# One DMA pipe in a list-scheduled transformer kernel's plan, tile rates by pairs of half entries, and layer 2 biases in one operation

## The chip, the cores and the metric

The kernel runs on one core of a Trainium2 chip. The metric is the device time of one launch in microseconds, smaller is better. All times are of that core. TensorE multiplies matrices into PSUM, VectorE (DVE), ScalarE (ACT) and GpSimd (POOL) work elementwise, and SyncE (SP) issues DMA transfers only.

## The reference

Two layers with the same weights are applied to 2048 tokens of width 448 in bf16. A layer is an attention block with 16 heads of 28 columns, and then a block of a token mixer and an MLP of width 1792; both add to their input:

```python
x = x + _A_ref(_layernorm(x), A_wqkv, A_wo)
x = x + _B_ref(_layernorm(x), B_w1, B_w2, B_w3, B_w4)
# twice
_A_ref: q, k, v = heads of x @ wqkv;  p = softmax(q k^T * 28**-0.5);  (p v) @ wo
_B_ref: h = gelu(layernorm(x) @ w1), its four column quarters moved by
        +1, -1, +2, -2 tokens;  x1 = x + h @ w2
        x1 + gelu(layernorm(x1) @ w3) @ w4
```

## The kernel before, in words

**A program from a planner.** The kernel is written as some hundred Python generators (their names begin with `t_`). Each yields operations with an engine, an estimated duration, and what they read and write, or waits for and gives signals. While the kernel is built, the class `Sched` (from line 185) simulates the engines with these estimates and picks one operation after the other (`run`, line 385); the class `Plan` (line 43) turns what each reads and writes into semaphore waits. What reaches the chip is one fixed list of instructions for each engine, which works through it in order. An estimate never runs on the chip, it only decides the order; any change of an estimate or of a priority can move operations anywhere in the program. For a DMA the planner knows the issuing engine's issue time (`iss`) and the time until the data are there (`t`); line 505 handles both.

**Attention.** Two layers are cut into 68 segments: the lists in `ORDER` have 8 entries for layer 1 and 9 for layer 2, each a stretch of queries (512 or 256 of them) against a stretch of key tiles, and each is done for four groups `g` of four heads. Two neighbouring segments, `si // 2`, make half an entry; there are 34 such pairs. The scores of one 128-key tile, one head and 512 columns fill one PSUM bank; there are 2048 such tiles. `t_scores` (line 1474) gives them to TensorE (matmul at line 1353) in units of three and two tiles alternately: banks 0 to 2, then banks 3 and 4. `t_exp` (line 1576) lets ScalarE take the exponential of a unit in one instruction (line 1591) out of PSUM into the ring `PT`. A unit may be scored when the exponential two units before it is through. `t_pv` (line 1603) multiplies the result with the values (matmuls recorded at line 802). The wider projections and the output matrices go through a helper that records them at line 811.

**Tiles for VectorE.** Some tiles are not given to ScalarE. VectorE takes their exponential by a polynomial in five operations: the first reads PSUM (`d_first`, line 1435), four more make up `d_chain` (lines 1462, 1464, 1466 and 1469). Such a tile comes in two kinds. A *ring* tile stands in bank 2, in the place of the third tile of a unit of three, so that ScalarE's exponential of this unit has two tiles; the unit that uses bank 2 next waits until VectorE has read it (`dx`). Any other VectorE tile is scored into one of the two banks kept for miscellaneous work (6 and 7), beside a full unit. How many there are is set by `R_RATE` (ring) and `D_RATE`, which have one rate per layer and query chunk. A rate is asked for at lines 1476 to 1508: a tile some 5 to 8 key blocks ahead is taken while the segment's count is below rate x blocks x 4, VectorE's planned load is low and buffers are free.

**Softmax bias.** The exponent's shift comes from the keys' largest norm so far. `t_bias` (line 1288) computes it for one layer, one stretch of keys and one head group, in four small VectorE operations of 128x1 (one at line 1300); when an entry begins with later keys, `t_fct` (line 1311) and `t_db` (line 1321) compute the difference of two such biases and a factor for what was summed before, and `t_qp` (line 1370) adds the difference to the queries.

**Loads and transposes.** `t_load` (line 824) issues the inputs; on the POOL queue (records at lines 848 to 858) it loads `wo`, `w1` and `w2` when segment `LSEG[1]` starts and `w3`, `w4` when `LSEG[2]` starts. `t_setup2` (line 981) zeroes `wo_pad` on POOL when segment `LSEG[0]` starts. `load_xT` (line 1120) waits for four normalized token tiles in DRAM (`xnd`) and loads them transposed by one DMA on SP's queue (line 1123); `tr_dma` (line 1013, DMA at line 1015) does the same for one tile from SBUF. The transposed tokens `xT` feed the projections of queries, keys and values.

**Mixer and MLP.** `t_mixA` (line 1787) and `t_mixB` (line 1927) follow the output projection. ScalarE's gelu needs another table than its exponential, so a gelu among exponentials costs two table loads: it runs over seven blocks of 512 columns at once (line 2019, `vaug` 128x3584). `tanh_gelu` (line 1833) is the other way: GpSimd and VectorE form the argument, ScalarE takes a tanh from the exponential's table (line 1839), VectorE finishes it. `TANHW` says by layer and first tile of the chunk which of the two a chunk's MLP uses, 0 for gelu.

**Fillers.** `keep_pe_busy` (line 324) puts matmuls on constants into TensorE's list (line 2065) where the plan leaves the engine idle.

The program's last part is what depends on the last segments: output projection, mixer and MLP of the last tokens, and the stores (`t_final`, line 2059). `RANK` and `Q_LEAD` are the priorities of the projections, norms, mixers and MLPs, and the lead that a chunk's query projection gets over its first use.

## Time and profile before

| what | value |
| --- | --- |
| median of three runs (lowest, highest) | 1064.53 us (1062.19, 1065.12) |
| the profiled execution's own time | 1063.28 us |
| its span, first to last instruction | 1061.5 us |
| mean granted TensorE clock | 0.992 |
| busy: PE, DVE, ACT, POOL | 990.9, 680.6, 1007.3, 306.0 us |
| largest group on ACT (line 1591) | 802 instructions, 910.4 us |
| filler matmuls (line 2065) | 3212 |

The span is the time from the first to the last instruction of the profiled execution; its own time is 1.8 us longer. An engine's busy time is the sum of the stretches in which it ran anything. A group is written as line, engine, operation, output and input, with the number of instructions, their busy time, the mean duration of one in ns, and then the idle time ahead of them with what ended most of it. Such durations can overlap their neighbours on the same engine, so that count times mean may exceed the busy time. A row of the timeline has start, length, engine, and in brackets the wait that ended there. Where several places are compared, a table by stretches of the span gives each engine's busy time in them. SPq and POOLq are the queues in which these two engines issue DMAs.

### The profile page before, as it was taken

The page shows a single profiled execution, that of the slowest core. Times are in us where ns is not written, and L with a number is a line of the kernel's source. Part 1 is how long each engine was busy: PE and PEld are TensorE (multiplying, and loading weights), DVE is VectorE, ACT ScalarE, POOL GpSimd, SP SyncE. Part 2 cuts the span into 40 slices and gives each one's busy share as a digit, 9 for nine tenths or more (in the row PEclk, how much of TensorE's full clock was granted, in tenths as well). Part 3 has the DMA queues.
Part 4 walks back from the last instruction along what each step waited for, and adds up shares of the span by engine and source line. Part 5 has one row for each costly group of instructions (what it writes and reads, how often), then busy time and mean ns, then how long its engine had stood idle before and what let it go on. Part 6 is the DMA issues. An engine that isn't in the chain of part 4 may idle for free.

```text
span 1061.5 us, 35381 instructions
## 1 busy us (share of the span) xinstructions
PE 990.9 (93%) x15980; PEld 410.0 (39%) x15983; DVE 680.6 (64%) x1365; ACT 1007.3 (95%) x913; POOL 306.0 (29%) x507
## 2 busy tenths in 40 slices
PE   8898998999999999999999989998989999899998
PEld 4332342333424334434432333343333343444465
DVE  7674797788568757776457445747778536565442
ACT  7998999999999999999999999999999999999952
POOL 2342112434232304453234111103554300432111
PEclk9999999999999999999999999999999999999999
DMA  4547232402121103231132114334412110121000
GB/s 117 130 117 202 76 72 68 62 22 37 21 75 41 33 12 86 63 52 23 33 78 74 44 52 129 104 76 116 74 23 32 32 39 25 34 66 25 12 21 24
DMA packets 96443, 64.22 MB, mean 61 GB/s; under 512 B 68580, under 2 KB 85172, under 8 KB 96292
## 3 DMA queue, kind: packets, MB, share of 16 engines
q1 hardware_dynamic: 92916, 53.88, 21.1%
q0 software_dynamic: 3376, 8.09, 2.8%
q8 instruction: 125, 2.05, 0.8%
q14 instruction: 26, 0.21, 0.1%
HBM read 28.03 MB, written 16.76 MB: 42 GB/s over the span
## 4 chain that ended last, share of the span: by engine, by line
ACT 72%; PE 20%; DMA 3%; DVE 3%; issue 1%; SPq 1%; POOL 0%; DVEq 0%
ACT PT L1591 66%; PE ps L811 11%; PE ps L1353 4%; PE ps L802 3%; ACT h2T L2019 2%; DMA xT<-xnd 2%; ACT fb L1839 1%; PE ps L2065 1%; ACT L2019 1%; DMA xT<-xn 1%; ACT L1591 1%; DVE fb L1462 0%; DMA rT<-ub 0%; DMA PT<-in_A_wqkv_dram 0%; SPq L1015 0%
## 5 line engine op out<-in xcount | busy, mean ns | idle before, releaser
L1591 ACT ACTIVATE PT<-ps 128x1024 bf16<-128x1024 f32 (+1 forms) x802 | 910.4, 1340 | 15.5 <-PE ps L1353 14.8
L1353 PE MATMUL ps<-qT,kT 32*128 32x512 bf16 (+1 forms) x2560 | 315.2, 341 | 36.8 <-ACT PT L1591 28.4
L802 PE MATMUL ps<-PT,vaug 128*32 128x512 bf16 (+1 forms) x2491 | 250.9, 342 | 0.8 <-ACT PT L1591 0.5
L1353 PEld LDWEIGHTS ps<-qT,kT 32*128 32x128 bf16 x2560 | 80.6, 91 | 317.6 <-ACT PT L1591 285.1
L811 PE MATMUL ps<-xT,w 128*32 128x512 bf16 (+4 forms) x2368 | 160.9, 345 | 5.8 <-DMA xT<-xn 4.0
L2065 PE MATMUL ps<-ident 128*32 128x256 bf16 x3212 | 145.9, 279 | 4.2 <-DVE hT L1820 2.4
L802 PEld LDWEIGHTS ps<-PT,vaug 128*32 128x32 bf16 x2491 | 74.2, 95 | 93.4 <-issue 76.8
L2065 PEld LDWEIGHTS ps<-ident 128*32 128x32 bf16 x3212 | 90.8, 98 | 31.9 <-issue 13.1
L811 PE MATMUL ps<-w,h2T 128*32 128x448 bf16 x1288 | 90.5, 358 | 5.7 <-ACT h2T L2019 5.7
L1696 POOL TENSOR_TENSOR otn<-ub,fb 128x512 bf16<-128x512 f32 (+1 forms) x35 | 39.9, 1139 | 187.7 <-DMA fb<-rscr 187.7
L1998 DVE CAST h2T<-ps 128x384 bf16<-128x384 f32 (+1 forms) x84 | 52.2, 622 | 50.8 <-PE ps L811 50.0
L811 PEld LDWEIGHTS ps<-xT,w 128*32 128x32 bf16 (+1 forms) x2368 | 64.6, 96 | 50.1 <-issue 27.2
L1138 POOL TENSOR_TENSOR sq<-kT 128x512 bf16<-128x512 bf16 (+2 forms) x32 | 31.2, 981 | 94.7 <-DVE kT L1152 80.4
L1837 POOL TENSOR_TENSOR fb<-hT 112x512 f32<-112x512 bf16 (+1 forms) x36 | 37.8, 1054 | 61.7 <-DVE hT L1820 53.7
L811 PEld LDWEIGHTS ps<-w,h2T 128*32 128x32 bf16 x1288 | 36.0, 97 | 34.9 <-issue 15.2
L811 PE MATMUL ps<-xT,wk_pad 128*32 128x512 bf16 (+2 forms) x576 | 44.6, 366 | 3.1 <-DMA xT<-xnd 3.0
L1923 POOL TENSOR_TENSOR x_res<-x_res,x1b 128x448 f32<-128x448 f32 x32 | 38.2, 1199 | 32.1 <-DVE xn L1010 32.1
L1435 DVE TENSOR_SCALAR yd<-ps 128x512 int32<-128x512 f32 x43 | 29.5, 687 | 25.6 <-PE ps L1353 25.2
L1138 POOL TENSOR_TENSOR sq<-qT 128x512 bf16<-128x512 bf16 x28 | 30.6, 1100 | 43.2 <-DVE qT L1187 36.2
L811 PE MATMUL ps<-wo_pad,otn 128*32 128x448 bf16 x512 | 39.5, 356 | 2.9 <-DVE x_res L1750 1.6
L811 PE MATMUL ps<-w,hT 112*32 112x448 bf16 x512 | 41.2, 355 | 0.5 <-DVE x1b L1908 0.5
L811 PE MATMUL ps<-xT,wq_pad 128*32 128x512 bf16 x448 | 39.3, 388 | 1.4 <-DMA xT<-xnd 0.9
(183 smaller groups left out, 1190.3 us busy)
## 6 DMA issues: line engine op xcount, KB each, us to landing
uscr<-ub SPq DMA_DIRECT2D x28, 256.0 KB, 2.0
ub<-uscr SPq DMA_DIRECT2D x28, 256.0 KB, 4.0
fb<-rscr SPq DMA_DIRECT2D x24, 256.0 KB
xnd<-xn SPq DMA_DIRECT2D x28, 128.0 KB, 2.1
x_res<-in_A_x_dram POOLq DMA_DIRECT2D x16, 224.0 KB, 2.7
xd<-x_res SPq DMA_DIRECT2D x16, 224.0 KB, 2.9
x_res<-xd SPq DMA_DIRECT2D x16, 224.0 KB, 3.6
out_dram<-obf SPq DMA_DIRECT2D x16, 112.0 KB, 1.7
```

What stands on the lines that cost most here:

```text
L802: return lambda e: e.matmul(out=out, lhsT=lhsT, rhs=rhs, start=start, stop=stop, **kw)
L811: r.append(e.matmul(out=out[c:c + w, :], lhsT=lhsT[:, c:c + w], rhs=rhs, start=start, stop=stop, tile_position=(0, c)))
L1138: return both("sq", 0.15 + NW * 0.0018, 0.07 + NW * 0.00104, lambda e: e.tensor_tensor(out=sq[:, si, 0:NW], in0=src, in1=src, op=ALU.mult) ...
L1353: yield op("pe", (0.005 + NW * 0.00042) / nc_, lambda e, i=i, kc=kc, j=j, g=g, a=a, NW=NW, bank=bank: e.matmul(out=ps[:, bank, i * NW:(i + ...
L1435: yield op("dve", c_ps(512), lambda e: e.tensor_scalar(out=y, in0=ps[:, bi(bank), :], scalar1=SCALE * L2E * FS, scalar2=-126.0 * FS, op0=A ...
L1591: yield op("act", 0.06 + n * w * 0.000833, lambda e, bk=bk, s0=s0, n=n, w=w: e.activation(out=PT[:, s0:s0 + n, 0:w], in_=ps[:, bk[0]:bk[0] ...
L1696: yield both("otn", 0.2 + NW * 0.0021, 0.07 + NW * 0.00104, lambda e: e.tensor_tensor(out=otn[:, g, 0:NW], in0=u, in1=rb[:, 0:NW], op=ALU. ...
L1837: yield both("z2", 0.2 + NW * 0.00165, 0.07 + NW * 0.00104, lambda e: e.tensor_tensor(out=f, in0=z, in1=z, op=ALU.mult), hk, [fk])
L1923: yield both("xx", 1.2, 0.54, lambda e: e.tensor_tensor(out=X, in0=X, in1=X1, op=ALU.add), [xk, ("x1b", s)], [xk], deps=[nop_])
L1998: ev = op("dve", c_ps(m * NW), lambda e, hr=hr, pv=pv: e.tensor_copy(out=hr, in_=pv), reads=[("ps", bi(b))], writes=hk, touch=[b])
L2019: yield op("act", c_act(len(fr_) * NW), lambda e, v=v: e.activation(out=v, in_=v, func=ACT.Gelu_apprx_tanh), reads=allk, writes=allk, tab= ...
L2065: return [e.matmul(out=ps[32 * c:32 * c + 32, bi(b), 0:256].rearrange("p (a n) -> p a n", n=128), lhsT=ident[:, 32 * c:32 * c + 32], rhs=i ...
```

## The change

Four things are changed, and a number of settings with them.

- The planner gets one DMA pipe (`self.pipe`). A DMA with a service time `svc` occupies it for so long, one after the other, and its data arrive at the pipe's end or later; with `hold` (the transposing loads) the issuing queue is held until the pipe is free. Most DMAs get such a time, issue times are 0.4 instead of 0.35 (1.25 instead of 1.2 for `tr_dma`), and the weight loads' estimates fall from 8, 16 and 18 us to 5. The same `svc` argument is added to the stores of `xn`, `x` and `u`, to their loads and to the load of `rscr`, which are left out below.
- `R_RATE` and `D_RATE` are keyed by the pair of segments, `si // 2`, with new values; `DRATE`, which nothing calls, goes. `RPRIO`, the planner's priority for reading a ring tile, goes from 0.5 to 1, and the farthest key block ahead from 7 to 8 (`DHI`, exclusive, 8 to 9).
- In layer 2 the biases of all four head groups are computed together (`t_bias4`), and so are the differences in `t_fct`; in layer 1 `t_bias` of every head group 1 to 3 keeps its priority, and that of group 0 gets the highest for all stretches of keys.
- The weight loads of `t_load` wait for the signal that `wo_pad` has been zeroed (`woz`), and `LSEG` goes from (4, 7, 9) to (5, 5, 7).

`TANHW` gets one entry set, and all of `RANK` and most of `Q_LEAD` have new values.

```diff
@@ -502,8 +503,14 @@
             if kw.get("port"):
                 self.port[eng] = (start, t_end)
             if dma:
-                self.cur[eng] = start + kw.get("iss", 0.35)
+                svc = kw.get("svc", 0.0)
+                self.cur[eng] = start + kw.get("iss", 0.4)
                 t_end = start + kw.get("dma_time", 3.0)
+                if svc:
+                    if kw.get("hold"):
+                        self.cur[eng] = max(self.cur[eng], self.pipe)
+                    self.pipe = max(self.pipe, start + 1.2) + svc
+                    t_end = max(t_end, self.pipe + 1.2)
             else:
                 self.cur[eng] = t_end
...
@@ -535,21 +542,21 @@
...
-R_RATE = {(0, 0): 0, (0, 1): 0.03, (0, 2): 0.01, (0, 3): 0.02, (0, 4): 0, (1, 0): 0, (1, 1): 0, (1, 2): 0, (1, 3): 0.01, (1, 4): 0}
+R_RATE = {(0,): 0, (1,): 0.03, (2,): 0.06, (3,): 0.01, (4,): 0, (5,): 0, (6,): 0, (7,): 0, (8,): 0.05, (9,): 0.05, (10,): 0.04, (11,): 0.04, (12,): 0.02, (13,): 0.03, (14,): 0, (15,): 0, (16,): 0.04, (17,): 0.04, (18,): 0, (19,): 0, (20,): 0.02, (21,): 0.08, (22,): 0, (23,): 0, (24,): 0.04, (25,): 0.04, (26,): 0, (27,): 0, (28,): 0.01, (29,): 0.01, (30,): 0, (31,): 0, (32,): 0.03, (33,): 0.03}
 RLO = 5
 RHI = 7
-RPRIO = 0.5
+RPRIO = 1
...
-DHI = 8
+DHI = 9
...
-Q_LEAD = {(0, 1): 10, (0, 2): 5, (0, 3): 6, (1, 0): 4, (1, 1): 8, (1, 2): 5, (1, 3): 9}
-D_RATE = {(0, 0): 0.11, (0, 1): 0.1, (0, 2): 0.07, (0, 3): 0, (0, 4): 0, (1, 0): 0.005, (1, 1): 0.105, (1, 2): 0.03, (1, 3): 0.02, (1, 4): 0}
...
+Q_LEAD = {(0, 1): 12, (0, 2): 6, (0, 3): 6, (1, 0): 12, (1, 1): 18, (1, 2): 6, (1, 3): 8}
+D_RATE = {(0,): 0.14, (1,): 0.135, (2,): 0.14, (3,): 0.145, (4,): 0.14, (5,): 0.185, (6,): 0.14, (7,): 0.135, (8,): 0.12, (9,): 0.155, (10,): 0.08, (11,): 0.05, (12,): 0.015, (13,): 0, (14,): 0.005, (15,): 0, (16,): 0.025, (17,): 0, (18,): 0.07, (19,): 0.12, (20,): 0.025, (21,): 0.04, (22,): 0.125, (23,): 0.105, (24,): 0.025, (25,): 0.04, (26,): 0.07, (27,): 0.105, (28,): 0.03, (29,): 0.03, (30,): 0.065, (31,): 0.05, (32,): 0.065, (33,): 0.095}
...
-TANHW = {(0, 0): 0, (0, 3): 0, (0, 7): 0, (0, 11): 0, (0, 13): 0, (1, 0): 0, (1, 3): 0, (1, 7): 0, (1, 11): 0}
+TANHW = {(0, 0): 0, (0, 3): 0, (0, 7): 0, (0, 11): 1, (0, 13): 0, (1, 0): 0, (1, 3): 0, (1, 7): 0, (1, 11): 0}
 Sched.AGED = 0
 Sched.TARGET = 0.6
...
@@ -558,7 +565,7 @@
...
-LSEG = (4, 7, 9)
+LSEG = (5, 5, 7)
...
@@ -847,15 +850,16 @@
             yield from xload(12, 16, 9.0)
             wo_v = A_wo.rearrange("(g j d) n -> j d g n", g=4, j=4, d=DH)
             yield ("wait", ("segstart", LSEG[1]))
+            yield ("wait", ("woz",))
             for j in range(4):
-                yield dma("pool", lambda e, j=j: e.dma_start(out=wo_pad[32 * j:32 * j + DH, :, :], in_=wo_v[j]), reads=[("woz",)], writes=[(("wo_pad",), j)], t=8.0, iss=0.7)
-            yield dma("pool", lambda e: e.dma_start(out=w1[:, 0:3, :], in_=B_w1[0:384, :].rearrange("(c p) n -> p c n", p=128)), writes=[(("w1",), 0)], t=8.0, iss=0.7)
-            yield dma("pool", lambda e: e.dma_start(out=w1[0:64, 3, :], in_=B_w1[384:448, :]), writes=[(("w1",), 1)], t=8.0, iss=0.7)
-            yield dma("pool", lambda e: e.dma_start(out=w2[:, :, :], in_=B_w2.rearrange("(c p) n -> p c n", p=112)), writes=[("w2",)], t=8.0, iss=0.7)
+                yield dma("pool", lambda e, j=j: e.dma_start(out=wo_pad[32 * j:32 * j + DH, :, :], in_=wo_v[j]), reads=[("woz",)], writes=[(("wo_pad",), j)], t=5.0, svc=0.35, iss=0.7)
+            yield dma("pool", lambda e: e.dma_start(out=w1[:, 0:3, :], in_=B_w1[0:384, :].rearrange("(c p) n -> p c n", p=128)), writes=[(("w1",), 0)], t=5.0, svc=1.2, iss=0.7)
+            yield dma("pool", lambda e: e.dma_start(out=w1[0:64, 3, :], in_=B_w1[384:448, :]), writes=[(("w1",), 1)], t=5.0, svc=0.2, iss=0.7)
+            yield dma("pool", lambda e: e.dma_start(out=w2[:, :, :], in_=B_w2.rearrange("(c p) n -> p c n", p=112)), writes=[("w2",)], t=5.0, svc=1.4, iss=0.7)
             yield ("wait", ("segstart", LSEG[2]))
-            yield dma("pool", lambda e: e.dma_start(out=w3[:, 0:3, :], in_=B_w3[0:384, :].rearrange("(c p) n -> p c n", p=128)), writes=[(("w3",), 0)], t=16.0, iss=0.7)
-            yield dma("pool", lambda e: e.dma_start(out=w3[0:64, 3, :], in_=B_w3[384:448, :]), writes=[(("w3",), 1)], t=16.0, iss=0.7)
-            yield dma("pool", lambda e: e.dma_start(out=w4[:, :, :], in_=B_w4.rearrange("(c p) n -> p c n", p=128)), writes=[("w4",)], t=18.0, iss=0.7)
+            yield dma("pool", lambda e: e.dma_start(out=w3[:, 0:3, :], in_=B_w3[0:384, :].rearrange("(c p) n -> p c n", p=128)), writes=[(("w3",), 0)], t=5.0, svc=4.9, iss=0.7)
+            yield dma("pool", lambda e: e.dma_start(out=w3[0:64, 3, :], in_=B_w3[384:448, :]), writes=[(("w3",), 1)], t=5.0, svc=0.6, iss=0.7)
+            yield dma("pool", lambda e: e.dma_start(out=w4[:, :, :], in_=B_w4.rearrange("(c p) n -> p c n", p=128)), writes=[("w4",)], t=5.0, svc=4.9, iss=0.7)
 
         def t_setup():
             yield op("dve", 0.1, lambda e: e.memset(ones_f[:, :], 1.0), writes=[("ones_f",)])
...
@@ -981,6 +985,7 @@
         def t_setup2():
             yield ("wait", ("segstart", LSEG[0]))
             yield op("pool", 2.0, lambda e: e.memset(wo_pad[:, :, :], 0.0), writes=[("woz",)])
+            yield ("sig", ("woz",))
             yield op("dve", 0.2, lambda e: e.memset(w1[64:128, 3, :], 0.0), writes=[(("w1",), "z")])
             yield op("dve", 0.5, lambda e: e.memset(w3[64:128, 3, :], 0.0), writes=[(("w3",), "z")])
             yield op("pool", 0.3, lambda e: e.memset(shf[:, :], 0.0), writes=[("shf", t) for t in range(NT)])
...
@@ -1121,7 +1126,7 @@
             for t in range(t0, t0 + n):
                 yield ("wait", ("xnd", L, t))
             yield dma("sp", lambda e: e.dma_start_transpose(out=xv(xt)[:, :, 0:128 * n], in_=xnd[128 * t0:128 * (t0 + n), :]),
-                      reads=[("xnd", t) for t in range(t0, t0 + n)], writes=[(("xT", xt), i) for i in range(4)], t=TRL_T, iss=2.2)
+                      reads=[("xnd", t) for t in range(t0, t0 + n)], writes=[(("xT", xt), i) for i in range(4)], t=TRL_T, svc=1.02 * n, hold=True, iss=2.2)
 
 
...
@@ -1303,6 +1308,24 @@
                      reads=[("bcb", L, p, g), (("cols",), 1)], writes=[("bc29", L, p, g)])
             yield ("sig", ("bc", L, p, g))
 
+        def t_bias4(L, p):
+            yield ("wait", ("rtn",))
+            for g in range(4):
+                for c in range(p):
+                    yield ("wait", ("k", L, g, c))
+            src, sk = kmaxc[:, L, :, 0], [("kmaxc", L, g, 0) for g in range(4)]
+            if p > 1:
+                yield op("dve", 0.14, lambda e: e.reduce_max(out=k2[:, L, p, :], in_=kmaxc[:, L, :, 0:p], axis=AX.X),
+                         reads=[("kmaxc", L, g, c) for g in range(4) for c in range(p)], writes=[("k2", L, p, g) for g in range(4)])
+                src, sk = k2[:, L, p, :], [("k2", L, p, g) for g in range(4)]
+            yield op("dve", 0.13, lambda e: e.tensor_tensor(out=sc[:, 5, :], in0=src, in1=RTN, op=ALU.mult), reads=sk + [("sc", 0)], writes=[("sc", 5)], two=True)
+            yield op("dve", 0.13, lambda e: e.tensor_scalar(out=bcb[:, L, p, :], in0=sc[:, 5, :], scalar1=WSH, scalar2=None, op0=ALU.add),
+                     reads=[("sc", 5)], writes=[("bcb", L, p, g) for g in range(4)])
+            yield op("dve", 0.13, lambda e: e.tensor_scalar(out=bc29[:, L, p, :], in0=bcb[:, L, p, :], scalar1=M29, scalar2=None, op0=ALU.mult),
+                     reads=[("bcb", L, p, g) for g in range(4)] + [(("cols",), 1)], writes=[("bc29", L, p, g) for g in range(4)])
+            for g in range(4):
+                yield ("sig", ("bc", L, p, g))
+
         PI = {}
         for L_ in range(2):
             for i_, k_ in enumerate(sorted({(ext_of(L_, a_), ext_of(L_, b_)) for (ch_, a_, b_) in ORDER[L_] if a_ > 0})):
...
@@ -1310,13 +1333,29 @@
 
         def t_fct(L, p, pp):
             i = PI[L, (pp, p)]
+            fexp = op("act", 0.25, lambda e: e.activation(out=fct[:, L, i, :], in_=dbc[:, L, i, :], func=ACT.Exp, scale=SCALE),
+                     reads=[("dbc", L, i)], writes=[("fct", L, i)], tab="exp")
             for g in range(4):
-                yield ("spawn", t_db(L, p, pp, g), 1)
+                if L == 0:
+                    yield ("spawn", t_db(L, p, pp, g), 1)
+                    continue
+                yield ("wait", ("bc", L, p, g))
+                yield ("wait", ("bc", L, pp, g))
+            if L == 0:
+                for g in range(4):
+                    yield ("wait", ("db29", L, i, g))
+                yield fexp
+                yield ("sig", ("fct", L, i))
+                return
+            yield op("dve", 0.13, lambda e: e.tensor_tensor(out=dbc[:, L, i, :], in0=bcb[:, L, p, :], in1=bcb[:, L, pp, :], op=ALU.subtract),
+                     reads=[("bcb", L, q_, g) for q_ in (p, pp) for g in range(4)], writes=[("dbc", L, i)], two=True)
+            yield op("dve", 0.13, lambda e: e.tensor_scalar(out=db29[:, L, i, :], in0=dbc[:, L, i, :], scalar1=M29, scalar2=None, op0=ALU.mult),
+                     reads=[("dbc", L, i), (("cols",), 1)], writes=[("db29", L, i, g) for g in range(4)])
             for g in range(4):
-                yield ("wait", ("db29", L, i, g))
-            yield op("act", 0.25, lambda e: e.activation(out=fct[:, L, i, :], in_=dbc[:, L, i, :], func=ACT.Exp, scale=SCALE),
-                     reads=[("dbc", L, i)], writes=[("fct", L, i)], tab="exp")
+                yield ("sig", ("db29", L, i, g))
+            yield fexp
             yield ("sig", ("fct", L, i))
+
 
         def t_db(L, p, pp, g):
...
@@ -1491,7 +1529,7 @@
                     if si > si0 + DSEG or si >= len(segs):
                         return None
                     L, ch, g = segs[si][0:3]
-                    rate = rates.get((L, ch), 0)
+                    rate = rates.get((si // 2,), 0)
                     if not rate:
                         return None
                     js = [j for j in range(4) if (si, kb, j) not in home and j not in used]
...
@@ -2078,8 +2116,11 @@
             for (ch, a_, b_) in ORDER[L]:
                 ext.setdefault(ext_of(L, b_), ext_of(L, a_))
             for e_ in sorted(ext):
+                if L == 1:
+                    SC.spawn(t_bias4(L, e_), 1)
+                    continue
                 for g in range(4):
-                    SC.spawn(t_bias(L, e_, g), 0 if (L, e_, g) == (0, 1, 0) else 1)
+                    SC.spawn(t_bias(L, e_, g), 0 if g == 0 else 1)
             for (e_, pe_) in sorted({(ext_of(L, b_), ext_of(L, a_)) for (ch, a_, b_) in ORDER[L] if a_ > 0}):
                 SC.spawn(t_fct(L, e_, pe_), 1)
             for si in range(len(segs)):
```

21 lines of the change are left out of this document (10 added, 11 removed).

## The prediction

> **What bounds the kernel now.** I read the page first: the busy shares, then the chain of work that ended last, then the costliest group.
>
> ```profile
> span 1061.5 us, 35381 instructions
> ...
> PE 990.9 (93%) x15980; PEld 410.0 (39%) x15983; DVE 680.6 (64%) x1365; ACT 1007.3 (95%) x913; POOL 306.0 (29%) x507
> ...
> ACT 72%; PE 20%; DMA 3%; DVE 3%; issue 1%; SPq 1%; POOL 0%; DVEq 0%
> ...
> L1591 ACT ACTIVATE PT<-ps 128x1024 bf16<-128x1024 f32 (+1 forms) x802 | 910.4, 1340 | 15.5 <-PE ps L1353 14.8
> ```
>
> ScalarE is busy for 95% of the span and is 72% of the chain; 910.4 of its 1007.3 us are the 802 exponentials of line 1591. TensorE's 93% is no second bound: the program holds 3212 filler matmuls (line 2065), of which more below. So a change is worth what it takes from ScalarE's work or from its idle time. By shape, ScalarE's groups are:
>
> ```profile
> L1591 ACT ACTIVATE PT<-ps 128x1536 bf16<-128x1536 f32 x383 | 599.2, 1564 | 10.2 <-PE ps L1353 9.6
> L1591 ACT ACTIVATE PT<-ps 128x1024 bf16<-128x1024 f32 x419 | 470.5, 1135 | 5.2 <-PE ps L1353 5.2
> ...
> L1839 ACT ACTIVATE fb<-fb 112x512 f32<-112x512 f32 x24 | 16.1, 692 | 0.0
> ...
> L2019 ACT ACT_TABLE_LOAD x8 | 10.3, 1283 | 0.1
> L1591 ACT ACT_TABLE_LOAD x7 | 9.0, 1283 | 0.1
> ...
> L2019 ACT ACTIVATE vaug<-vaug 128x3584 bf16<-128x3584 bf16 x2 | 6.4, 3192 | 0.0
> ```
>
> The means overlap their neighbours (383 x 1.564 + 419 x 1.135 is 1075, not 910.4), so I need what one instruction moves the next by. The two shapes differ by one 512-column tile and 1.564 - 1.135 = 0.43 us. With b for two tiles and b + 0.43 for three, 802 b + 383 x 0.43 = 910.4 gives b = 0.93 and 1.36.
>
> Idle time comes next. A table by stretches (columns: stretch, its length, busy us of PE, PEld, DVE, ACT, POOL, granted clock, DMA share, GB/s) over the places where the exponentials waited:
>
> ```profile
> 16.00:37.00 21.00, 17.32 (x245) 6.40 (x246) 18.97 (x50) 17.92 (x20) 3.81 (x6) 1.00 0.16 57
> 81.00:101.00 20.00, 16.68 (x218) 5.43 (x219) 7.80 (x17) 15.87 (x15) 2.17 (x3) 0.91 0.85 241
> 160.00:186.00 26.00, 23.15 (x287) 6.94 (x280) 20.50 (x34) 24.05 (x23) 7.57 (x8) 0.93 0.19 57
> 205.00:213.00 8.00, 6.37 (x55) 1.38 (x55) 5.15 (x10) 5.87 (x7) 2.34 (x2) 0.79 0.59 118
> 300.00:324.00 24.00, 21.57 (x315) 8.19 (x313) 16.16 (x24) 21.81 (x22) 9.17 (x12) 0.93 0.33 89
> 646.00:660.00 14.00, 13.53 (x217) 5.45 (x210) 5.08 (x10) 14.00 (x14) 1.58 (x4) 1.00 0.59 157
> 660.00:674.00 14.00, 12.22 (x160) 4.17 (x162) 11.50 (x31) 14.00 (x13) 3.22 (x4) 1.00 0.24 76
> ```
>
> Length minus ACT busy is what ScalarE lost: 3.1, 4.1, 2.0, 2.1 and 2.2 us in the first five rows, nothing in the last two. The second row has the DMA engines 85% busy; the timelines of POOL, SP and PE tell why:
>
> ```profile
> 81.02 1.12 POOL L858 DMA_DIRECT2D w<-in_B_w_dram  x1
> ```
> ```profile
> 86.05 7.14 SPq L1123 DMA_TRANSPOSE xT<-xnd  x1
> ```
> ```profile
> 95.47 0.41 PE L811 MATMUL ps<-xT,wk_pad 128*32 128x512 bf16 x4 [3.00 <-DMA xT<-xnd]
> ```
> ```profile
> L1123 SPq DMA_TRANSPOSE xT<-xnd x12: 1304/2730/7137, 35.7 to 730.7; - x12
> ```
>
> The w4 load goes out at 81.0; the transposing load of the fourth token chunk starts at 86.0 and takes 7.14 us to issue against a median of 2.73; TensorE, which takes its work in order, then stands 3.0 us before the first matmul that reads it, with the scores queued behind.
>
> **The change, part by part.** All times are in the plan that the kernel makes while it is built; on the chip only orders and instructions differ. The DMA pipe, the new issue times and the waits of `t_load` are such planning. I therefore compared the built orders, engine by engine.
>
> 1. *Tiles moved off ScalarE.* With `R_RATE` and `D_RATE` by pairs of half entries, the built order holds 359 exponentials of three tiles and 444 of two: 24 fewer and 25 more. That is 25 x 0.93 - 24 x 1.36 = **-9.4 us**. It is 22 tiles more for VectorE (83 instead of 61). 42 instead of 18 of them are "ring" tiles, scored into bank 2 in the place of ScalarE's third tile; those in other banks fall from 43 to 41. What VectorE pays per tile:
>
> ```profile
> L1435 DVE TENSOR_SCALAR yd<-ps 128x512 int32<-128x512 f32 x43 | 29.5, 687 | 25.6 <-PE ps L1353 25.2
> L1469 DVE SCALAR_TENSOR_TENSOR PD<-yd,PD 128x512 int16<-128x512 int16 x40 | 28.5, 713 | 0.7
> L1462 DVE SCALAR_TENSOR_TENSOR fb<-yd 128x512 f32<-128x512 uint16 x38 | 28.3, 746 | 2.2 <-POOL otn L1696 1.8
> L1464 DVE SCALAR_TENSOR_TENSOR fb<-fb,yd 128x512 f32<-128x512 f32 x38 | 27.0, 712 | 0.4
> ...
> L1466 DVE TENSOR_SCALAR PD<-fb 128x512 bf16<-128x512 f32 x45 | 20.3, 453 | 0.6
> ...
> L1300 DVE TENSOR_SCALAR bcb<-k,sc 128x1 bf16<-128x1 f32 x20 | 4.3, 216 | 0.6
> ```
>
> The five steps sum to 0.69 + 0.75 + 0.71 + 0.45 + 0.71 = 3.3 us, so 22 tiles add 73 us to 680.6: about 72% of the new span, beside the exponentials. Split by stages of the built order, no stage gets more than five extra tiles. The cover is VectorE's idle third; without it, rival B.
>
> The Trainium skill (Advanced Engine Details and Errata, Mode Summary under VectorE Performance Modes) says that VectorE's second SBUF port is shared with GpSimd, and that two-port operations and GpSimd block each other. The trace agrees where it can be seen: line 1462 averages 0.75 us above, where its copies on other buffers take 0.69. By that rule the added chains would cost some tenths each, still beside the exponentials, and the sum would stay.
>
> 2. *One gelu becomes tanh.* `TANHW[0, 11] = 1` removes a gelu of 128x3584 (3.19 us) and the two table loads around it (2 x 1.28), in all 5.8; it adds seven tanh of 512 columns. In the chain of waits two neighbours together move the engine by 1.04 us,
>
> ```profile
> 436.57 1.04 ACT fb L1839 x2
> ```
>
> so seven cost 3.6: **-2.1 us**. With the full mean of 0.69 it would be -0.9. VectorE and GpSimd get seven more operations each (about 0.7 and 1.2 us each), off the path.
>
> 3. *Loads and transposes.* I followed waits and queue order through both programs and counted each instruction's place in exponentials already required (one is 910.4/802 = 1.14 us). The w3/w4 loads move from exponential 48 to 34, some 16 us earlier, so w4's end moves from before 94 to before about 80, ahead of the fourth transposing load (54 before, 51 now). The first matmul that needs that load stood 6 exponentials behind it and now stands 9. The fifth such load goes from 105 to 90; the small transposes behind the stall at 205 get 9 exponentials of room instead of 5. So I count the 4.1, 2.0 and 2.1 us of three rows as gone: -8.2. From both sides: 0 if the collision only moves, since wo, w1 and w2 now go out at exponential 26, beside the third transposing load; -13.5 if all five rows go. I take the nearest rows. The explicit wait for the zeroed `wo_pad` adds no stall: memset and loads stand on POOL in this order anyway.
>
> 4. *Layer 2 biases in one op.* 52 small operations of 0.2 us (the L1300 row) become 16 wider ones, 36 x 0.21 = 7.6 us of VectorE that nothing waits for. Its price: all four head groups wait for the last. Before the second and third use there are 46 and 26 exponentials of room, before the last (keys 11 to 15) only 3, 3.4 us, where a chain of some six operations of 0.2, a 0.35 update and a score stand. Nothing, or about 2.4 us if one tile's steps (0.7 each) stand in front: I take +1.2. Parts 3 and 4 together: **-7.0 us**.
>
> 5. *The tail.* After the last exponential ScalarE has little left and TensorE sets the end:
>
> ```profile
> 1026.33 3.50 PE L811 MATMUL ps<-xT,w 128*32 128x256 bf16 x112
> 1029.64 2.46 PE L811 MATMUL ps<-w,hT 112*32 112x448 bf16 x48
> ...
> 1040.75 0.84 PE L2065 MATMUL ps<-ident 128*32 128x256 bf16 x24
> 1041.42 9.28 PE L811 MATMUL ps<-xT,w 128*32 128x384 bf16 x224
> ```
>
> Behind the last score the new order has 36 more matmuls of 512 columns (9.28/224 scaled by 512/384: 55 ns), 32 more of w2 (51 ns), 12 more of 256 columns (31 ns) and no filler (24 x 35 ns): 2.0 + 1.6 + 0.4 - 0.8 = **+3.2 us**. Between 1.5, if part of it lies under waits for the gelu, and 4.5, if the shorter cover behind the last output projection (92 matmuls, 4.7 us) doesn't hide the layer norm.
>
> Sum: -9.4 - 2.1 - 7.0 + 3.2 = -15.3. The profiled execution took 1063.3 us (span 1061.5 and 1.8 around it), so 1048.0; the median of the three runs lies 1.2 us above it: **1049 us**.
>
> **The rivals.**
> A, the stalls come back elsewhere: the planner's DMA model hides none of them, or the earlier loads hold the third transpose as w4 held the fourth. For it: 802 exponentials lost time in only a few places, and each place is an accident of order. Against: the room grew at nearly every tight transpose. 1049 + 8.2 = **1057**.
> B, slower: VectorE comes late to the ring tiles. TensorE may not score into bank 2 again before VectorE has read it, and the next exponentials queue behind. The place is each of the 24 added ring tiles; the price is the read, 0.69, up to 1.4 with one chain step in front. From 15.3/24 = 0.64 us each the gain is gone; at 1.0 each, 1049 + 24 = **1073**. Against: behind the 18 ring tiles of before, ScalarE's pace shows almost no loss, and the waits of the exponentials sum to 14.8 us in all.
> C, slower: the clock. The new order has 404 fewer fillers. The rows above show 0.91 and 0.79 where TensorE waited. Without filler (3212 x 35 ns) its busy time is 990.9 - 112 = 879 us; at 0.79 throughout that is 1112 us and TensorE is the bound; it passes 1063 from a mean clock of 0.83 down. Against: 660:674 has no filler at all and clock 1.00. The Trainium skill (TensorE: Matmul & The Clock Gate, What's actually happening) says that the array drops to half its clock after an idle window of about 3.4 us. By that rule fewer fillers matter only where TensorE stands idle that long; the trace agrees in so far as the row with the 3.0 us wait is among the slow ones.
> D, better: the losses at 16:37 and 300:324 shrink too, **1043**.
>
> **How the numbers follow.** Forecast (1044 to 1054) 0.62, A 0.18, B 0.08, C 0.03, D 0.09. This kernel's measurement can tell about 0.3%, 3.2 us, from no change. Faster by more: forecast, D and nearly all of A, 0.88. Within: the edge of A and a mild B, 0.04. Slower: the rest of B, and C, 0.08. The range 1041 to 1061 takes in D, the forecast and A with its bounds; B and C stay out.
>
> **What would show it.** Right: the exponentials' group busy about 901 us; ACT idle before line 1591's successor well under 15; a transposing load near 80 us that issues in under 3 us; the last exponential near 990, and 55 to 56 us behind it. Wrong: DVE named as releaser of scores, a granted clock under 0.98, or a new wait of the scores near exponential 541 (the last bias). The forecast falls if part 3 moves its collisions instead of clearing them.

## The result and the profile after

| | before | after |
| --- | --- | --- |
| first timing, median of four runs | 1063.36 us | 1048.62 us (1043.21 to 1053.57) |
| ratio, 95% interval | | 0.9858 (0.9815 to 0.9900) |
| second timing on another occasion, median | 1062.29 us | 1045.15 us |
| ratio, 95% interval | | 0.9837 (0.9822 to 0.9852) |
| profiled execution | 1063.28 us | 1043.21 us |
| its mean granted TensorE clock | 0.992 | 1.000 |

The change makes the kernel 1.4 to 1.6% faster, 15 to 17 us. The forecast was 1049 us: 15.3 off the profiled execution of before (1063.3), and 1.2 on top because the median lay that much above it. At the same mean clock of 0.995, executions took 1060.6 to 1062.8 us before (second timing) and 1046.9 to 1050.1 after (three in both timings), so the gain isn't one of the clock. The page of the changed kernel, span and busy times first, then the exponentials' group, then ScalarE's groups by shape:

```profile
span 1041.4 us, 34669 instructions
...
PE 972.0 (93%) x15579; PEld 397.3 (38%) x15579; DVE 742.2 (71%) x1450; ACT 995.2 (96%) x921; POOL 319.6 (31%) x514
...
L1629 ACT ACTIVATE PT<-ps 128x1024 bf16<-128x1024 f32 (+1 forms) x803 | 900.9, 1323 | 7.2 <-PE ps L1391 6.8
```
```profile
L1629 ACT ACTIVATE PT<-ps 128x1536 bf16<-128x1536 f32 x359 | 559.7, 1559 | 3.9 <-PE ps L1391 3.5
L1629 ACT ACTIVATE PT<-ps 128x1024 bf16<-128x1024 f32 x444 | 487.6, 1132 | 3.3 <-PE ps L1391 3.3
...
L2057 ACT ACTIVATE vaug<-vaug 128x3584 bf16<-128x3584 bf16 x1 | 3.2, 3202 | 0.0
```

The exponentials (now line 1629) fell from 910.4 to 900.9 us, the idle time ahead of them from 15.5 to 7.2. A table by three stretches, cut at the first and the last exponential, shows the whole account. Before, then after; columns are the stretch, its length, busy us of PE, PEld, DVE, ACT, POOL, clock, DMA share, GB/s:

```profile
0.00:16.02 16.02, 13.04 (x230) 7.43 (x231) 11.47 (x51) 11.44 (x17) 5.30 (x18) 1.00 0.67 192
16.02:1008.75 992.73, 929.20 (x14626) 371.44 (x14628) 650.72 (x1277) 975.88 (x870) 291.12 (x468) 0.99 0.25 60
1008.75:1061.50 52.75, 48.63 (x1124) 31.17 (x1124) 18.43 (x38) 20.02 (x29) 9.60 (x21) 1.00 0.07 23
```
```profile
0.00:15.83 15.83, 13.18 (x239) 7.35 (x243) 11.47 (x51) 11.43 (x16) 5.32 (x18) 1.00 0.69 195
15.83:986.90 971.07, 907.61 (x14164) 357.54 (x14164) 709.64 (x1354) 963.43 (x875) 300.73 (x469) 1.00 0.25 61
986.90:1041.40 54.50, 51.21 (x1182) 32.36 (x1180) 21.14 (x46) 20.32 (x31) 13.52 (x27) 0.99 0.09 26
```

Between the first and the last exponential ScalarE works 12.4 us less and idles 9.2 us less (16.85 to 7.64); the tail is 1.75 us longer, the start 0.2 shorter: -20.1 us in these two executions. The lost time of the second row of the prediction is gone:

```profile
78.00:98.00 20.00, 17.99 (x229) 6.07 (x225) 14.50 (x35) 19.93 (x19) 5.17 (x5) 1.00 0.36 97
```
```profile
82.16 2.03 SPq L1128 DMA_TRANSPOSE xT<-xnd  x1
```

ScalarE is busy for 19.93 of these 20 us, and the fourth transposing load issues in 2.03 us instead of 7.14. The places of the prediction's rows at 160, 205 and 300, which come 5 to 10 us earlier now:

```profile
150.00:180.00 30.00, 27.09 (x411) 10.41 (x409) 24.26 (x42) 30.00 (x28) 9.65 (x12) 1.00 0.27 72
...
200.00:208.00 8.00, 8.00 (x109) 2.34 (x101) 5.90 (x9) 7.83 (x8) 2.23 (x4) 1.00 0.48 57
...
290.00:314.00 24.00, 23.53 (x328) 8.03 (x328) 17.94 (x34) 23.91 (x24) 10.16 (x14) 1.00 0.20 62
```

ScalarE loses 0.0, 0.2 and 0.1 us there, instead of 2.0, 2.1 and 2.2. The prediction hadn't counted on the last of them.

### The profile page after: what moved, and what is told of

The parts are those of the page before. It is cut to its first block, busy times and chain, and to the rows that moved or that the text cites. A ratio compares the mean times of both kernels' runs of the same rounds, so it can differ in the third digit from the quotient of the medians.

```text
span 1041.4 us, 34669 instructions
## 1 busy us (share of the span) xinstructions
PE 972.0 (93%) x15579; PEld 397.3 (38%) x15579; DVE 742.2 (71%) x1450; ACT 995.2 (96%) x921; POOL 319.6 (31%) x514
## 4 chain that ended last, share of the span: by engine, by line
ACT 74%; PE 19%; DVE 3%; DMA 2%; issue 0%; POOL 0%; SPq 0%; DVEq 0%
ACT PT L1629 67%; PE ps L814 11%; PE ps L1391 4%; ACT h2T L2057 3%; PE ps L805 3%; ACT fb L1877 2%; ACT L1629 1%; ACT L2057 1%; DMA fb<-rscr 1%; DMA rT<-ub 0%; DMA xT<-xn 0%; DMA PT<-in_A_wqkv_dram 0%; DVE PD L1507 0%; ACT sq L1140 0%; DVE yd L1473 0%
## 5 line engine op out<-in xcount | busy, mean ns | idle before, releaser
L1629 ACT ACTIVATE PT<-ps 128x1024 bf16<-128x1024 f32 (+1 forms) x803 | 900.9, 1323 | 7.2 <-PE ps L1391 6.8
L814 PE MATMUL ps<-xT,w 128*32 128x512 bf16 (+4 forms) x2368 | 154.8, 340 | 3.4 <-DVE h2T L2036 1.5
L2103 PE MATMUL ps<-ident 128*32 128x256 bf16 x2808 | 130.5, 278 | 1.8 <-POOL ident L895 1.5
L814 PE MATMUL ps<-w,h2T 128*32 128x448 bf16 x1288 | 88.3, 355 | 7.3 <-ACT h2T L2057 7.0
L2103 PEld LDWEIGHTS ps<-ident 128*32 128x32 bf16 x2808 | 79.5, 97 | 27.8 <-issue 11.3
L814 PEld LDWEIGHTS ps<-xT,w 128*32 128x32 bf16 x2368 | 63.3, 95 | 49.1 <-issue 21.4
L2036 DVE CAST h2T<-ps 128x384 bf16<-128x384 f32 (+1 forms) x84 | 52.0, 619 | 34.3 <-PE ps L814 33.9
L1473 DVE TENSOR_SCALAR yd<-ps 128x512 int32<-128x512 f32 x62 | 42.5, 688 | 35.5 <-PE ps L1391 35.3
L814 PEld LDWEIGHTS ps<-w,h2T 128*32 128x32 bf16 x1288 | 34.3, 96 | 36.7 <-issue 14.7
L814 PE MATMUL ps<-xT,wq_pad 128*32 128x512 bf16 x512 | 43.4, 382 | 0.1
L1507 DVE SCALAR_TENSOR_TENSOR PD<-yd,PD 128x512 int16<-128x512 int16 x59 | 41.4, 703 | 1.2
L814 PE MATMUL ps<-xT,wk_pad 128*32 128x512 bf16 (+2 forms) x512 | 41.4, 362 | 0.2 <-DVE kmaxc L1170 0.2
```

The lines of the kernel that those rows point to most:

```text
L814: r.append(e.matmul(out=out[c:c + w, :], lhsT=lhsT[:, c:c + w], rhs=rhs, start=start, stop=stop, tile_position=(0, c)))
L1473: yield op("dve", c_ps(512), lambda e: e.tensor_scalar(out=y, in0=ps[:, bi(bank), :], scalar1=SCALE * L2E * FS, scalar2=-126.0 * FS, op0=A ...
L1507: yield op(D_[3][0], D_[3][1], lambda e: e.scalar_tensor_tensor(out=pdt.bitcast(I16), in0=hi, scalar=128.0, in1=pdt.bitcast(I16), op0=ALU. ...
L1629: yield op("act", 0.06 + n * w * 0.000833, lambda e, bk=bk, s0=s0, n=n, w=w: e.activation(out=PT[:, s0:s0 + n, 0:w], in_=ps[:, bk[0]:bk[0] ...
L2036: ev = op("dve", c_ps(m * NW), lambda e, hr=hr, pv=pv: e.tensor_copy(out=hr, in_=pv), reads=[("ps", bi(b))], writes=hk, touch=[b])
L2103: return [e.matmul(out=ps[32 * c:32 * c + 32, bi(b), 0:256].rearrange("p (a n) -> p a n", n=128), lhsT=ident[:, 32 * c:32 * c + 32], rhs=i ...
```

## The experiments

Theory: the gain consists of fewer exponentials, of ScalarE's lost stretches, and of little else, and belongs to the built order. Rivals: the lost stretches are drops of the clock that come and go; VectorE's ring tiles or the missing fillers take something back; each part carries its own price whatever the order.

In some kernels the built order is *held*: the planner's finished list is taken as it is, one thing in it is edited, and the waits are derived again from what is read and written. All others are planned anew. Differences to the changed kernel are taken between the ratios (1% is 10.6 us), with 0.9837 for the changed kernel.

### Both kernels once more

No edit.

> The kernel before, unchanged, for a second trace and the granted clock of every run. In its first trace ScalarE lost 27.8 us against its own pace between the exponentials, nearly all at a few places, and the four-microsecond stretches with a clock below 0.97 were exactly at those places (96, 164 to 172, 208, 316 to 324, 916 to 924). Theory 1 (order): these losses belong to the built order, so a second trace has them at the same exponentials, 25 to 30 us in all, and the time is 1060 to 1065. Rival (clock): only the losses at 52 and 96 us return, which stand behind transposing loads; the others (about 10 us) are what single stretches at half clock cost, and they move to other places or go. Then time falls by about 1 us for each 0.001 of clock.

Measured: 1062.37 us, ratio 0.9998 (0.9988 to 1.0009). The second to fifth rows of the prediction's table again, in the second trace, half a microsecond later or a microsecond earlier:

```profile
81.50:101.50 20.00, 16.63 (x218) 5.38 (x221) 7.72 (x17) 15.78 (x16) 2.21 (x3) 0.91 0.84 240
160.50:186.50 26.00, 23.08 (x284) 7.10 (x284) 20.43 (x35) 23.99 (x23) 7.80 (x8) 0.93 0.21 60
205.50:213.50 8.00, 6.14 (x76) 1.72 (x74) 5.56 (x10) 7.05 (x8) 2.56 (x3) 1.00 0.60 117
299.00:323.00 24.00, 21.80 (x330) 8.26 (x328) 18.12 (x26) 22.98 (x23) 9.63 (x13) 1.00 0.33 94
```

The wait behind the transposing load is the same (4.2 us lost, 4.1 before), and so is the loss at 160 (2.0 in both, at a clock of 0.93 in both). The last two lost 2.1 and 2.2 us at a clock of 0.79 and 0.93; at 1.00 they lose 0.95 and 1.0. Instead the clock drops at two places where it had been full. In stretches of 4 us, the first trace and then the second:

```profile
208.00:212.00 4.00, 4.00 (x31) 0.74 (x29) 3.97 (x8) 3.20 (x4) 0.13 (x1) 0.57 0.32 72
...
972.00:976.00 4.00, 4.00 (x99) 2.14 (x91) 1.61 (x4) 4.00 (x6) 1.33 (x2) 1.00 0.02 4
```
```profile
208.00:212.00 4.00, 3.49 (x42) 0.83 (x34) 3.97 (x8) 4.00 (x5) 0.00 (x0) 1.00 0.43 97
...
972.00:976.00 4.00, 4.00 (x82) 2.11 (x78) 1.18 (x3) 2.99 (x4) 1.08 (x2) 0.80 0.01 4
```

Cut at its edges, such a drop is 3.41 us at half the clock; this is the one of the first trace at 208:

```profile
208.38:211.79 3.41, 3.41 (x26) 0.62 (x21) 3.38 (x7) 2.61 (x4) 0.00 (x0) 0.50 0.23 51
```

Each trace of this kernel has five of them before the tail. Three stand at the same places in both (at 96, 168 and 919), two moved (from 208 and 318 to 32 and 970). So both are partly right: the place of a wait belongs to the order, but about half of what the rows at 205 and 300 lost goes with a drop of the clock that another execution has elsewhere. The Trainium skill (TensorE: Matmul & The Clock Gate, What's actually happening) says that the window in which the hardware watches TensorE's activity runs freely and isn't tied to the kernel's start; the two moved drops agree, and the three others show that the order has a part in it too.

> The changed kernel, unchanged, for a second trace and the clock of every run. Its four runs so far took 1043.2, 1047.1, 1050.1 and 1053.6 us at clocks of 1.000, 0.995, 0.995 and 0.989; the trace is of the first. Theory 1 (order): 1045 to 1052, ratio near 0.986, and the waits stand where they stood, 19 us in all. Rival (clock): the time follows the clock, from 1043 at 1.000 to 1053 at 0.989, and a trace with a clock below 1 shows additional waits of the exponentials at stretches of half clock, at places where the first trace has none.

Measured: 1045.15 us (1043.78 to 1046.90), ratio 0.9837 (0.9822 to 0.9852); the profiled execution had a clock of 0.998. The order's waits stand where they stood. One exponential wait is new, at a drop of the clock; the stretch in the first trace, then here:

```profile
112.00:116.00 4.00, 3.37 (x58) 1.47 (x54) 2.05 (x9) 4.00 (x5) 1.04 (x1) 1.00 0.37 131
```
```profile
112.00:116.00 4.00, 3.48 (x49) 1.51 (x49) 2.49 (x11) 4.00 (x4) 1.04 (x1) 0.70 0.41 132
116.00:120.00 4.00, 3.95 (x56) 1.42 (x50) 1.30 (x3) 3.08 (x4) 0.00 (x0) 0.87 0.02 4
```

ScalarE loses 0.9 us of the second four. This is the only drop before the tail; the first trace has none. That the slower executions of the changed kernel (1053.6 us at a clock of 0.989) have more of them fits their clocks, but those were not profiled.

### The weight loads alone, both ways (order held)

In the kernel before, the loads of w3 and w4 moved up:

```diff
+    # w3 and w4 go out after the Nth exponential; N = 34
+            if n == 34:
+                out += ld
```

> The kernel before, every instruction in the same order, except that the three loads of w3 and w4 stand behind exponential 34 on GpSimd's queue instead of 48 (so also ahead of wo, w1 and w2). Theory of the prediction (the w4 load holds up the fourth transposing load): that load issues in under 4 us instead of 7.1, the wait of the exponentials at 96 to 100 us (4.5 us in all) goes, and the time falls by 3 to 5 us, ratio 0.996. Rival 1: the loads now collide with the third transposing load (issued near 55 us) and the wait at 52 us (1.8) grows instead by 2 to 4: no change of the time. Rival 2: the long issue has another cause: the wait at 96 stays.

Measured: 1057.27 us, ratio 0.9956 (0.9940 to 0.9972), so 4.7 us faster (3 to 6 by the interval). The wait at 96 us is gone; a shorter one, 1.2 us, came where the loads now go out. The two stretches, then the one that was at 160, and SP's timeline:

```profile
60.00:72.00 12.00, 10.61 (x108) 2.74 (x105) 8.90 (x21) 10.78 (x11) 5.21 (x8) 0.86 0.91 313
81.00:101.00 20.00, 19.67 (x278) 6.65 (x270) 10.38 (x20) 19.96 (x19) 2.10 (x3) 1.00 0.44 98
```
```profile
156.00:182.00 26.00, 21.99 (x287) 6.97 (x287) 21.49 (x36) 24.80 (x24) 7.97 (x9) 1.00 0.25 69
```
```profile
87.33 1.96 SPq L1123 DMA_TRANSPOSE xT<-xnd  x1
```

The moved wait itself is worth 2.9 us (4.1 less 1.2). Another 0.8 comes from the stretch at 160, which has no drop here and loses 1.2 us instead of 2.0.

In the changed kernel the loads moved down to exponential 48:

```diff
+            if n == 48:
+                out += ld
```

> The mirror: the changed kernel, same order, with the loads of w3 and w4 behind exponential 48 instead of 34 on GpSimd's queue. They then go out about 2 us ahead of the fourth transposing load (82.2 us in the first trace). Theory of the prediction: this load's issue grows from 2.0 to some 7 us and a wait of 2 to 4 us appears at about 92 to 96 us; ratio to before 0.986 to 0.988 instead of 0.984. Rival (room): the changed order has 9 exponentials of room there instead of 6 and absorbs it: the issue gets long but no wait appears, ratio 0.984.

Measured: 1047.32 us, ratio 0.9861 (0.9846 to 0.9875), 2.5 us more than the changed kernel; the two intervals overlap by a little, so the trace has to decide. The collision is back, on SP's timeline and in ScalarE's stretch:

```profile
81.89 8.11 SPq L1128 DMA_TRANSPOSE xT<-xnd  x1
```
```profile
81.00:101.00 20.00, 17.07 (x198) 5.38 (x197) 11.78 (x25) 17.52 (x17) 4.16 (x4) 0.91 0.81 200
```

8.11 us of issue, 2.5 us of lost exponentials: the theory holds, and less is lost than the 4.1 of before, as the larger room of the new order would have it. (This trace also loses 2.0 us at a drop of the clock at 762 to 770, where the changed kernel's two traces have none.) The two runs change nothing but the place of three instructions, and the wait goes and comes with it: the cause of this one wait is shown. The loads and transposes behind the rows at 160 and 205 were not moved by themselves.

### The ring tiles' reads doubled (order held)

```diff
+        if o.eng == "dve" and "d_first" in o.fn.__qualname__ and ("ps", 2) in o.args[0]:
+            out.append(o)
```

> The changed kernel, same order, but VectorE reads each of the 42 ring tiles out of bank 2 twice (42 more instructions of 0.69 us, 29 us). If the read of a ring tile ends the wait of the next scores (rival B): up to 42 x 0.69 + 42 x 0.13 = 34 us more, 1075 to 1083. If VectorE's idle third covers it, as the prediction counts: less than 5 us more, 1045 to 1054. A figure between, 10 to 20 us, would say that the ring is near its limit and that doubling the ring tiles again would cost.

Measured: 1064.93 us (1061.61 to 1072.90), ratio 1.0033 (1.0012 to 1.0053): about 21 us more than the changed kernel, 0.5 per ring tile: a little above the figure between. Counted from start to start against ScalarE's own pace (1.33 us after a unit of three tiles, 0.90 after one of two), the 42 exponentials of ring units and the ones behind them lose 2.9 us together in the changed kernel and 11.5 here. From one before to four behind each, it is 17.4 us more here, and in the rest of the kernel 12 more. This is the profiled execution, the slowest of the ten (1072.9 us); much of its loss stands where the clock drops:

```profile
976.00:984.00 8.00, 8.00 (x78) 3.50 (x80) 5.06 (x12) 5.08 (x5) 3.37 (x9) 0.57 0.00 0
```

The drops don't explain the whole: at a mean clock of 0.995 this kernel took 1061.6 and 1063.6 us, the changed one 1046.9 to 1050.1. Who waited for the first reads (line 1473):

```profile
  PEld ps L1391: 5.7, 13
...
  PE ps L1391: 1.8, 6
```

Line 1391 is the scores. In the changed kernel's answer to the same question they don't appear at all. So the ring tiles are covered as they are, but the cover is thinner than one read: 0.7 us later on each, and the whole gain is gone.

### The fillers (order held)

All 2808 left out, then every second one:

```diff
+    return [o for o in ops if not (o.eng == "pe" and o.plan[1].get("w") == 0.107)]
```

> The changed kernel with every other instruction in the same order on every engine and all 2808 filler matmuls left out of TensorE's list. If the clock hangs on the fillers (rival C of the prediction): mean clock below 0.96 and a time above 1060. If the real work keeps the clock up: 1040 to 1050 at a clock of 0.99 or more, with TensorE busy about 975 - 98 = 875 us. My guess is in between: clock 0.96 to 0.98 and 1055 to 1070, since single idle stretches of a few microseconds are then not filled any more.

Measured: 1081.82 us, ratio 1.0178 (1.0162 to 1.0193), clock 0.905. The page's busy times, and one stretch:

```profile
PE 966.4 (89%) x12771; PEld 334.8 (31%) x12771; DVE 740.8 (69%) x1450; ACT 1002.9 (93%) x921; POOL 321.2 (30%) x514
```
```profile
230.00:250.00 20.00, 17.26 (x129) 4.09 (x129) 13.44 (x26) 15.20 (x16) 4.35 (x5) 0.66 0.05 12
```

The clock does hang on the fillers. TensorE's busy time hardly falls (972.0 to 966.4): the real matmuls take longer and fill what the fillers left (without their 130.5 us in the changed kernel it would be about 841).

> The changed kernel, same order, with every second filler left out (1404 instead of 2808). Without any filler it took 1081.8 us at a clock of 0.905, 36.7 us more than with all. If the loss goes with the number of missing fillers, half of it appears: 1063 to 1065, clock near 0.95, and the 404 fillers that the change itself drops would be worth about 5 us. If the clock only falls where a whole stretch of some microseconds has too little work: well under half, 1048 to 1056 with a clock of 0.97 to 0.99. My guess is the second.

Measured: 1048.35 us (1046.84 to 1057.29), ratio 0.9888 (0.9845 to 0.9931), clock 0.993. Half the fillers are worth 3 to 5 us (1 to 10 by the interval), not half of 36. So the price is not by the piece; that it comes where a whole stretch gets too little work fits, but is argued. What the 404 fillers cost that the change itself drops was not tried by itself; by these two runs it is small.

### One part at a time (planned anew)

The new rates alone, in the kernel before (both tables, and their key):

```diff
-                    rate = rates.get((L, ch), 0)
+                    rate = rates.get((si // 2,), 0)
```

> One part alone: the kernel before with only the two rate tables, their key and the wider reach of nothing else: R_RATE and D_RATE by pairs with the new values. The built order has 363 exponentials of three tiles and 435 of two (before 383 and 419). By the prediction's first term: -20 x 1.36 + 16 x 0.93 = -12.3 us, 1050. Rival: the values fit only the order they came with; in the old order VectorE is late where it has other work and the waits take the gain back or more: 1062 or above, with more than 28 us of losses between the exponentials and VectorE behind them. My guess: 1060 to 1085, since nothing else was shifted to make room.

Measured: 1107.27 us, ratio 1.0419 (1.0402 to 1.0436): 45 us slower with 20 exponentials of three tiles fewer. ScalarE's timeline at the change of layers:

```profile
563.08 0.40 ACT L1839 ACTIVATE fb<-fb 112x256 f32<-112x256 f32 x1
588.41 3.19 ACT L2019 ACTIVATE vaug<-vaug 128x3584 bf16<-128x3584 bf16 x1 [24.93 <-DVE vaug L1998]
...
616.14 0.21 ACT L1317 ACTIVATE fct<-dbc 128x4 f32<-128x4 f32 x1 [23.24 <-DVE dbc L1326]
620.86 4.62 ACT L1591 ACTIVATE PT<-ps 128x1536 bf16<-128x1536 f32 x4 [4.51 <-PE ps L1353]
```

ScalarE stands for 53 us. It has run out of exponentials of layer 1, and those of layer 2 need keys whose tokens come late out of the last mixer and MLP of layer 1. The chain of waits of the same execution, three rows of it:

```profile
594.20 2.53 DMA xnd<-xn
596.83 5.31 DMA kT<-xnd
...
602.18 3.85 PE ps L811 x64
```

The normalized tokens are stored at 594, loaded transposed, and projected from 602 on. Not VectorE at the tiles, as the rival had it, but the layer boundary; why the last mixer and MLP come later than before was not traced. The price of the tiles was right and unimportant here: the exponentials' group is busy for 898.0 us, 12.4 less than before, and 12.3 were expected.

The old rates in the changed kernel:

```diff
-R_RATE = {(0,): 0, (1,): 0.03, (2,): 0.06, (3,): 0.01, ...
+R_RATE = {(0,): 0, (1,): 0, (2,): 0, (3,): 0, ...
```

> The changed kernel with the values of the old rate tables written out for the pairs, all else as changed. The built order has 386 exponentials of three tiles and 416 of two. By the first term: 27 x 1.36 - 28 x 0.93 = +10.7 us against the changed kernel, 1056, if nothing else moves. Rival: the order around it is rebuilt as well and adds losses of its own, 1060 to 1070; or fewer tiles on VectorE let it be earlier elsewhere, 1050.

Measured: 1059.41 us, ratio 0.9979 (0.9970 to 0.9988), 15 us more than the changed kernel. Between first and last exponential ScalarE is busy for 974.4 us, 11.0 more (10.7 expected), and idles 11.8, 4.1 more: one wait of 2.7 us at 306 is the largest.

```profile
15.50:1001.66 986.16, 924.22 (x14691) 370.28 (x14693) 640.40 (x1232) 974.38 (x875) 299.21 (x472) 0.99 0.24 61
```

Here, with the surroundings that fit, the tile count carries most of it.

The gelu set back:

```diff
-TANHW = {..., (0, 11): 1, ...}
+TANHW = {..., (0, 11): 0, ...}
```

> The changed kernel with TANHW[0, 11] set back to 0: one gelu of 128x3584 and two table loads instead of seven tanh. The built order has 361 exponentials of three tiles and 442 of two, as changed but for two. By the prediction's price of this part: +2.1 us, 1047. Rival (order): every engine's list is rebuilt around it, and the values of the other settings no longer fit; then 1055 to 1075, with new holes of ScalarE rather than longer instructions.

Measured: 1069.05 us, ratio 1.0072 (1.0055 to 1.0088): 25 us more than the changed kernel, not 2. ScalarE's work up to the last exponential is 3.7 us more (967.1), 0.9 of it for two units of three tiles in the place of two; that is 2.8 for the gelu itself.

The biases of layer 2 by head group again, and the differences in `t_fct` with them:

```diff
-                if L == 1:
-                    SC.spawn(t_bias4(L, e_), 1)
-                    continue
```

> The changed kernel with the layer 2 biases computed head group by head group again. By the prediction's price: 36 more small VectorE operations (7.6 us off the path) and no common wait, so between 0 and -1.2 us, 1044 to 1046. Rival (order): the rebuilt lists cost 10 to 25 us, 1055 to 1070, although the same work is done in the same number of exponentials (360 and 443).

Measured: 1068.54 us, ratio 1.0076 (1.0042 to 1.0110), also 25 us more (the profiled execution took 1075.7). And the old priorities, with everything else as changed:

```diff
-RANK = {('q', 0, 1): 1.02, ...
+RANK = {('q', 0, 1): 1.1, ...
```

> The changed kernel with the old values of RANK and Q_LEAD, that is only priorities. The instructions are the same in kind and the exponentials nearly (362 of three tiles, 438 of two). If the prediction's parts carry the gain by what they remove: 1045 to 1050. Rival (order): the gain is only there in the order that these priorities make; then 1060 to 1085, with the added loss as ScalarE idle time at the change of layers and behind late projections.

Measured: 1080.21 us, ratio 1.0171 (1.0154 to 1.0188), 35 us more. In these three the rival is right. Where the time is, by the stretch behind the last exponential (gelu set back, biases by head group, old priorities, in this order):

```profile
997.00:1067.10 70.10, 63.80 (x1516) 43.27 (x1506) 32.48 (x72) 21.41 (x33) 20.22 (x42) 1.00 0.09 25
```
```profile
998.50:1073.90 75.40, 70.40 (x1592) 44.93 (x1592) 30.16 (x65) 23.94 (x45) 16.58 (x32) 1.00 0.08 22
```
```profile
1013.53:1078.20 64.67, 60.91 (x1394) 38.05 (x1387) 21.86 (x47) 21.58 (x37) 13.55 (x27) 1.00 0.12 28
```

The tail is 70.1, 75.4 and 64.7 us long instead of 54.5. What stands in it is read from TensorE's groups of these stretches: in the changed kernel, with the biases by head group, and with the old priorities

```profile
L814 PE MATMUL ps<-xT,w 128*32 128x256 bf16 (+3 forms) x530 | 19.4, 299 | 0.0
```
```profile
L814 PE MATMUL ps<-xT,w 128*32 128x256 bf16 (+3 forms) x768 | 31.9, 315 | 0.0
```
```profile
L814 PE MATMUL ps<-xT,w 128*32 128x256 bf16 (+3 forms) x660 | 26.5, 315 | 0.4 <-DVE xT L1041 0.4
```

238 and 130 matmuls of `xT` with mixer and MLP weights more, which ran beside exponentials in the changed kernel. With the gelu set back the normalization of the last segments stands there for four head groups and not for one (with the biases by head group as well):

```profile
L805 PE MATMUL ps<-rT,selq 8*128 8x128 f32 x4 | 0.7, 296 | 0.0
```
```profile
L805 PE MATMUL ps<-rT,selq 8*128 8x128 f32 x16 | 2.8, 296 | 0.0
```

And its chain of waits runs for 12 us, from 1024.7 to 1036.7, through a residual and a layer norm on VectorE and GpSimd alone, where the changed kernel's chain is on TensorE from 994.7 to 1038.5. The first and the last operation on VectorE:

```profile
1024.68 1.27 DVE x1b L1946 x2
...
1035.37 1.32 DVE xn L1015
```

The last exponential comes 10, 12 and 27 us later as well; with the old priorities ScalarE idles 34.3 us before it, 14.3 of them in one wait for scores at 567 us, again near the change of layers.

## Why the prediction was right

The sum (-15.3) and the mechanism held, and each term can be read in the traces. The biases and the tail were sized too high, the loads and transposes came to their sum partly by luck, and one reason was missing.

- *Tiles off ScalarE*, -9.4: measured -9.5 (910.4 to 900.9). VectorE's busy time rose by 62 us to 71% of the span; its five lines for the tiles rose by 69 (199.6 to 268.7), where 73 were counted. One reading was too broad, without effect on the sum: the mean of 0.75 us of line 1462 comes from one instruction of 3.05 us among 38, beside GpSimd's work; the median is 0.68, as on the other buffers.
- *One gelu as tanh*, -2.1: the rest of ScalarE's work before the last exponential fell by 12.4 - 9.5 = 2.9 us, and setting the gelu back gave 2.8. The price of the work was about right; that the setting can't be undone alone for this price was not foreseen.
- *Loads and transposes*, -8.2: the idle time fell by 9.2 in the first pair of traces (16.85 to 7.64) and by 8.9 in the second. The row of 4.1 us is shown by moving the three loads alone (4.7 us in all, 2.9 of it this wait). The rows of 2.0 and 2.1 were the weak ones. I took them whole, from one trace: without a drop of the clock the order before loses 1.2 and 0.9 there, so of the 8.2 about 6 belonged to the order. That the term came out even so has two reasons that I hadn't counted: the loss at 300 went as well (1.0 at full clock), and the changed kernel's two traces have none and one of the drops where those of before have five each. Why they have fewer, no run shows.
- *Biases*, +1.2: most of this loss didn't come. The answer for the updates of the queries (line 1413), which read the biases, names who waited for them: scores, once, for half a microsecond:

```profile
  PEld ps L1391: 0.5, 1
```

- *The tail*, +3.2: measured 1.75 in both pairs. TensorE's work grew by 51.21 - 48.63 = 2.6 us, but its idle time there fell from 4.1 to 3.3.

In the profiled pair the change brings 20.1 us, not 15.3: 0.8 from the gelu, 2.2 from the stalls and the bias, 1.5 from the tail, 0.3 from the rest. That the first median lay 0.4 us from the forecast is partly luck: its four executions ran at clocks of 0.989 to 1.000, the profiled one at 1.000. The second timing, 1045.15, lies 3.9 below the forecast and inside its range.

Of the rivals, A (stalls come back elsewhere, 1057) didn't occur: the longest wait of an exponential in the changed kernel's first trace is 1.8 us. B's mechanism exists, and a delay of one read of each ring tile takes the whole gain (1064.9, not B's 1073), but the order leaves enough room. C's mechanism exists too: without fillers the clock is 0.905 (I had taken 0.79), and half of them keep nearly all of it. A drop doesn't need TensorE to stand idle throughout: in the 3.41 us ahead of the five drops of the first trace of before it was busy for 0.4 to 2.3, and ahead of one in the second for 3.3. I had priced a filler at 35 ns by a single row; the 3212 of before are busy for 145.9 us, 45 ns each. D came in part: the loss at 300 went, and that at 16 fell from 3.1 to 1.9; its time, 1043, is that of the best executions.

The missing reason: I priced the settings' work and took the order as given. That was right only because I had the built order to count in. Rates, gelu, biases and priorities, undone one at a time, cost 15, 25, 25 and 35 us, 100 together, for a change that brings 17. The sizes of such a sum belong to one order; they are no prices of the settings.

## What to carry to other kernels

Where a planner builds the order, count in the built lists (instructions, queue places, room before each wait, work behind the last instruction of the bounding engine), and don't price a setting by its work. To show a cause, hold the order and move one thing: three moved loads gave 4.7 us, and the wait could be watched going and coming, while the edits that were planned anew cost 15 to 45 us, most of it elsewhere than at the thing edited (only the old rates cost about what their work does). When a wait in a profile stands at a drop of the clock, look at a second execution before you count on the whole of it.
